# Seven block products (Strassen) for the projection to V in the second layer of a two-layer attention and token-mixing kernel

## The chip, the core and the metric

The kernel runs on one core of a Trainium2 chip. A core has five engines with a queue of instructions each: TensorE (PE, matrix products; its weight loads are listed as PEld), VectorE (DVE), ScalarE (ACT), GpSimd (POOL) and SyncE (SP), which here only issues DMAs. Each engine takes its instructions in the order of the program, and semaphores tie the engines to each other. The metric is the device time in microseconds (us) of one execution, as the median of several runs.

## The reference

Two layers with the same weights; each is sliding-window attention (32 heads of 32, 8 keys at a distance of 2) and a token-mixing MLP.

```python
def _A_ref(x, wqkv, wo):
    qkv = (x @ wqkv).reshape(B, S, 3, H, Dh)        # S = 2048, D = 1024
    ...                                             # windowed softmax attention
    return o @ wo

def _B_ref(x, w1, b1, w2, b2):
    h = _layernorm(x)
    u = _gelu(jnp.einsum("bsd,sf->bdf", h, w1) + b1)  # F = 3584
    y = jnp.einsum("bdf,fs->bds", u, w2) + b2
    return y.transpose(0, 2, 1)

x = x + _A_ref(_layernorm(x), wqkv, wo)             # layer one
x = x + _B_ref(_layernorm(x), w1, b1, w2, b2)
x = x + _A_ref(_layernorm(x), wqkv, wo)             # layer two
x = x + _B_ref(_layernorm(x), w1, b1, w2, b2)
```

The change concerns the last third of `x @ wqkv`, the projection to V, in layer two.

## The kernel before

The 2048 tokens are held as two sets of 1024, even and odd positions (`c = 0, 1`), of eight tiles of 128 tokens each (`i = 0..7`); `cols(c, i)` are the columns of a tile in `hT`, the normalised input with the 1024 features on the partitions (eight blocks `kt`). The stages of a layer follow each other: projection to V, then attention unit by unit (projection to Q and K, scores, mask, values), output projection, the first product of the MLP (`gemm1`) and the second (`gemm2f` in layer one, `gemm2s` in layer two). The two products of the MLP are already done as seven block products each, in half precision (f16), with their weights scaled by a power of two that comes from a bound of the absolute weights. Such a bound is found per partition, stored to DRAM and read back as a broadcast to all partitions (`share_w2`: a small reduction on DVE, the store `mxw` and the broadcast `bcw` on SP); `power_w2` reduces the broadcast on DVE to the scale and its inverse.

- **The order of work.** `chain_(engine, f, ...)` writes out the order on an engine: every call comes behind the engine's call before. `in_order` does the same for PE. In layer one's start, `start_up` has a list for each engine (`pe`, `act`, `dve`, `sp`).
- **V in layer one** runs in `start_up`, tile by tile, with the normalisation of the input. **V in layer two** is `v_proj`: for each tile (c, i) and each half n of the 1024 outputs, eight matmuls 128x128 by 128x512 into a bank of PSUM, then a copy on ACT to `v[c][i]`.
- **`gemm2f`** (layer one). For `i = 0, 1` the products are plain (`tokens`), with the weights `w(0)` and `w(1)`; during these the bounds of the later weights are found: `refill` loads pieces of `w2` into free room of `hT`, ACT's `bounds` makes a bound of each piece, `share(4)` and `share(6)` spread them, and `scaled`, `mix`, `t2` and `t4` make the sums for `i = 2`. For `i = 2..7` there are seven products of 14 matmuls each, with a bank move on ACT between some of them. After each `i` come `quarter` (DVE: scale, add to the residual), `aggregate` (statistics; the store to `xb`), `root` (ACT: reciprocal root) and `normalise` (DVE, then a transposing DMA into `hT`). `seam(0)` at `i = 6` loads the V weights `wv`, `seam(1)` at `i = 7` the first weights of Q and K.
- **Buffers.** `wp` has nine weight buffers, `gop` 14 (the hidden values `g` of the MLP fill them until the sixth product of `i = 7`), `x2p` six; PSUM has eight banks (two `m`, four `s`, two `a`).
- `zero_fill` clears `Pm` (the masked probabilities) and both `qB` on DVE, once in `start_up` and once behind `gemm2f`.

## Time and profile before

| | |
|---|---|
| median of 3 runs | 1207.44 us (1207.15 to 1207.7) |
| the profiled execution | 1208.3 us, span of its instructions 1206.5 us |
| busy, share of the span | PE 98%, DVE 62%, ACT 56%, POOL 10% |
| granted clock of PE | 1.0 over the span |
| V of layer two | 608.4 to 663.8 us |
| `gemm2f`, `i = 0, 1` (`tokens`) | from 432.7 us |
| `gemm2f`, `i = 2` to `7` | from 481.0 us |

The span is the time from the first to the last instruction that the profile shows; times in the prediction are counted from its start. In lines of the order of time, the columns are the start, the length, engine, line and operation, written tile `<-` read tiles, shapes, and in brackets the idle time of the engine before it with what ended it. A line of waits has the engine and what it waited for, the sum, the number of times, and the longest. L1125 is the line of the products of `gemm2f`, L1130 that of its moves on ACT, L1159 `quarter`, L1171 `aggregate`, L1175 `root`, L212 `normalise`, L692 the bounds on ACT, L658 to L661 `share_w2`, L611 any DVE tensor-tensor operation, L226 DMAs that `chain_` issues.

### The profile page before, as it was taken

The numbers are of one execution on the slowest core, as the hardware profiler recorded it, in microseconds if no ns is written. First come the engines' busy times: TensorE is split into PE (matmuls) and PEld (weight loads), VectorE is DVE, ScalarE is ACT, GpSimd is POOL, SyncE is SP. The second block draws the span as 40 slices with busy tenths as digits, with TensorE's granted clock in tenths as the row PEclk, the third lists the DMA queues.
The fourth block names the chain that finished last, engine by engine and source line by source line (L and its number), as shares of the span: only waits on it lengthen the run. The fifth ranks groups of instructions, "written<-read, shape, count | busy, mean of one in ns | idle before, by whom it ended". The sixth has DMA issues, their size and how long they took to land.

```text
span 1206.5 us, 20332 instructions
## 1 busy us (share of the span) xinstructions
PE 1188.3 (98%) x7865; PEld 551.6 (46%) x8004; DVE 751.8 (62%) x1451; ACT 671.2 (56%) x1136; POOL 125.8 (10%) x121
## 2 busy tenths in 40 slices
PE   9999999999999999999999999999999999999998
PEld 4444444444444444444444444444444444444444
DVE  7558887887777546866440688888612322784663
ACT  4457766578878776665433677754543434432332
POOL 0000000281000041000000000002811212100000
PEclk9999999999999999999999999999999999999999
DMA  8922233696776678966520232425855645165521
GB/s 236 157 63 71 79 106 95 211 277 167 205 210 169 206 197 196 223 175 163 160 53 1 65 86 67 121 92 166 279 157 161 199 150 162 48 192 140 157 70 36
DMA packets 248274, 174.01 MB, mean 144 GB/s; under 512 B 48240, under 2 KB 224496, under 8 KB 244848
## 3 DMA queue, kind: packets, MB, share of 16 engines
q1 hardware_dynamic: 248176, 172.69, 51.3%
q8 instruction: 63, 1.03, 0.4%
q14 instruction: 35, 0.29, 0.1%
HBM read 130.17 MB, written 30.43 MB: 133 GB/s over the span
## 4 chain that ended last, share of the span: by engine, by line
PE 94%; DMA 2%; DVE 2%; ACT 1%; issue 1%; DVEq 0%
PE m L400 18%; PE s L771 11%; PE m L516 9%; PE m L771 7%; PE s L975 7%; PE a L771 6%; PE m L385 5%; PE s L1125 4%; PE m L975 4%; PE s L289 3%; PE m L1125 3%; PE a L975 3%; PE s L597 2%; PE a L1125 2%; PE s L431 2%; PE s L1218 2%
## 5 line engine op out<-in xcount | busy, mean ns | idle before, releaser
L400 PE MATMUL m<-hT,wqk 128*128 128x512 bf16 x963 | 223.7, 379 | 6.2 <-issue 4.5
L447 DVE TENSOR_TENSOR Pm<-pc,band 32x640 bf16<-32x640 bf16 x256 | 123.6, 483 | 45.7 <-ACT pc L435 38.9
L400 PEld LDWEIGHTS <-wqk 128*128 128x128 bf16 x1024 | 95.3, 98 | 117.9 <-issue 10.7
L771 PEld LDWEIGHTS <-Sw 128*128 128x128 f16 x832 | 81.4, 98 | 99.4 <-issue 1.3
L516 PE MATMUL m<-wo,oT 128*128 128x512 bf16 x500 | 110.8, 379 | 0.9 <-issue 0.3
L771 PEld LDWEIGHTS <-w 128*128 128x128 f16 (+1 forms) x624 | 61.1, 98 | 73.6
L611 POOL TENSOR_TENSOR T<-h 128x512 f16<-128x512 bf16 x16 | 18.5, 1154 | 613.0 <-DMA xr<-xb 363.9
L411 DVE COPY qB<-qs 32x512 bf16<-32x512 bf16 x136 | 38.2, 281 | 66.3 <-ACT qs L407 63.3
L516 PEld LDWEIGHTS <-oT 128*128 128x128 bf16 x512 | 49.6, 98 | 60.6 <-issue 1.9
L435 ACT ACTIVATE pc<-s,shift 128x320 bf16<-128x320 f32 x128 | 60.9, 532 | 11.7 <-PE s L431 11.7
L771 PE MATMUL s<-T,Sw 128*128 128x512 f16 x288 | 66.2, 379 | 1.1 <-ACT s L780 1.1
L611 DVE TENSOR_TENSOR py<-pz,m 128x512 f32<-128x512 f32 x14 | 9.6, 687 | 91.2 <-PE m L771 62.8
L407 ACT CAST qs<-m 128x512 bf16<-128x512 f32 x64 | 37.5, 586 | 44.4 <-PE m L400 41.6
L404 ACT CAST kT<-m 128x512 bf16<-128x512 f32 x64 | 37.5, 586 | 41.8 <-PE m L400 38.8
L611 POOL TENSOR_TENSOR Pm<-g 128x512 f16<-128x512 bf16 x24 | 28.6, 1209 | 283.1 <-ACT Pm L692 164.3
L385 PE MATMUL m<-wv,hT 128*128 128x512 bf16 x251 | 55.2, 379 | 0.3
L523 DVE TENSOR_TENSOR xn<-m,xr 128x512 bf16<-128x512 f32 x64 | 44.1, 689 | 15.2 <-PE m L516 14.6
L771 PE MATMUL m<-T,Sw 128*128 128x512 f16 x224 | 52.9, 379 | 0.0
L771 PE MATMUL a<-h,w 128*128 128x512 bf16 x224 | 52.9, 379 | 0.0
L611 DVE TENSOR_TENSOR xs<-tq,xs 128x512 bf16<-128x512 f32 (+1 forms) x30 | 21.9, 732 | 49.7 <-ACT tq L1130 32.5
L556 ACT ACTIVATE h<-xn,bi,rs 128x1024 bf16<-128x1024 bf16 x32 | 39.7, 1241 | 23.2 <-DVE bi L542 23.2
L747 ACT ACTIVATE w<-w,cs 128x2048 f16<-128x2048 bf16 x26 | 51.8, 1997 | 0.0
(220 smaller groups left out, 2097.8 us busy)
## 6 DMA issues: line engine op xcount, KB each, us to landing
w<-in_B_w_dram SPq DMA_DIRECT2D x110, 512.0 KB, 6.0
sd<-Sw SPq DMA_DIRECT2D x13, 1024.0 KB, 8.2
Sw<-sd SPq DMA_DIRECT2D x13, 1024.0 KB, 4.9
wqk<-in_A_wqkv_dram SPq DMA_DIRECT2D x16, 512.0 KB, 5.0
xa<-xn SPq DMA_DIRECT2D x32, 256.0 KB, 2.9
xs<-xa SPq DMA_DIRECT2D x32, 256.0 KB, 3.6
Pm<-in_B_w_dram SPq DMA_DIRECT2D x26, 256.0 KB, 6.1
wo<-in_A_wo_dram SPq DMA_DIRECT2D x8, 512.0 KB, 6.2
```

The costliest lines, as they stand in the source:

```text
L385: nc.tensor.matmul(ps[:], lhsT=hT[:, kt, cols(c, i)], rhs=wv[kt // 2][:, kt % 2, n * 512:(n + 1) * 512], start=(kt == 0), stop=(kt == KD - 1))
L400: mm = nc.tensor.matmul(ps[:], lhsT=wts[part][:, kt, (g % 2) * P:(g % 2 + 1) * P], rhs=hT[:, kt, lo:lo + 512], start=(kt == 0), stop=(kt = ...
L435: nc.scalar.activation(out=pc[:, 2 * n:2 * n + 2].rearrange("p t h k -> p (t h k)"), in_=ss[n][:, 0:2 * HG * GW], func=ACT.Exp, scale=scal ...
L447: mm = nc.vector.tensor_tensor(out=Pm[rp, :, s0:s0 + HB, r * KG:r * KG + GW].rearrange("p h t k -> p t h k"), in0=pc[rp], in1=mk, op=ALU.mult)
L516: mm = nc.tensor.matmul(ps[:], lhsT=oT[g][:, cols(c, i)], rhs=wo[n][g // 4][:, g % 4, :], start=(g == 0), stop=(g == NG - 1))
L523: return nc.vector.tensor_tensor(out=xn[:, xs_], in0=pss_["o", n][:], in1=xr[:, xs_], op=ALU.add)
L556: last["ACT"] = nc.scalar.activation(out=h2[c][i][:], in_=xn[:], func=ACT.Identity, bias=t["bi"][:], scale=t["rs"][:])
L611: return eng.tensor_tensor(out=out, in0=a, in1=b, op=op)
L747: return nc.scalar.activation(out=w[:].bitcast(FP16), in_=w[:], func=ACT.Identity, scale=cs[:, fb + 1:fb + 2])
L771: r = nc.tensor.matmul(out, lhsT=lhs[:, k, :], rhs=rhs[k], start=start and k == 0, stop=stop and k == NI - 1, skip_group_check=True)
L975: r = nc.tensor.matmul(out, lhsT=lhs[k], rhs=rhs[k][:, cols_], start=start and k == 0, stop=k == K - 1, skip_group_check=True)
L1125: r = nc.tensor.matmul(out, lhsT=lhs[k], rhs=rhs[k], start=start and k == 0, stop=k == K - 1, skip_group_check=True)
```

## The change

`v_proj` gives way to a class `Sevens`. A pair of token tiles is (0, i) and (1, i): with the two halves of the 1024 features and the two halves of the 1024 outputs, a product of 2x2 by 2x2 blocks, done as seven products of four matmuls each. Two pairs are done in turns (a round), on four banks each. The sums of token blocks (`s_sum`, 512 elements a partition from `hT`, f16) go to tiles `Sv` from `gop`, those of weight blocks (`t_sum`, 1024 elements) to tiles `T2`, `T3`, `T4` from `wp`, and `T1` in place; all on DVE. ACT moves banks between the products and scales the four `wv` tiles to f16; DVE's `put` adds two results to a kept one.

The scale comes in layer one: `start_up` gives ACT eight `bound_wv` (one for each block of `wv`, behind evictions 6 to 13) and DVE `top_wv`. In `gemm2f`, `share_wv` (a store and a broadcast) goes to SP behind `load_w(1)`, and `power_wv` to DVE behind the first `corner_add`. At `i = 7` of `gemm2f` the scalings, `t_sum` and `s_sum` of the first two pairs are put between the steps. The `zero_fill` behind `gemm2f` is split: `Pm` is cleared in the second round, both `qB` in the third. `last_pe` is reset in layer one alone, so that PE's order runs on from V to Q and K in layer two.

```diff
@@ -328,9 +336,19 @@
+        def bound_wv(kt):
+            junk = x2("junk")
+            return nc.scalar.activation(out=junk[:], in_=wv[kt // 2][:, kt % 2, :], func=ACT.Abs,
+                                        accum_out=mxv[:, kt // 4, kt % 4:kt % 4 + 1])
+
+        def top_wv():
+            return nc.vector.tensor_reduce(out=mv2[:], in_=mxv[:], op=ALU.max, axis=AX.X)
+
         rs = [(R_, k) for k in range(9, NT)]
         for k in range(4, NT):
             act.append((E_, k))
+            if 0 <= k - 6 < KD:
+                act.append((bound_wv, k - 6))
             act += rs[:2]
...
         dve.append((zero_fill,))
         dve.append((cast_biases,))
+        dve.append((top_wv,))
...
-    def v_proj(v, c, i, wv, ns):
-        for n in ns:
-            ps = m_tile()
-            for kt in range(KD):
-                nc.tensor.matmul(ps[:], lhsT=hT[:, kt, cols(c, i)], rhs=wv[kt // 2][:, kt % 2, n * 512:(n + 1) * 512],
-                                 start=(kt == 0), stop=(kt == KD - 1))
-            nc.scalar.copy(out=v[c][i][:, n * 512:(n + 1) * 512], in_=ps[:])
+    def share_wv():
+        bcw["v"] = pcp.tile([P, P, 2], FP32, name="bcv", tag="pc")
+        nc.sync.dma_start(out=mxvd[:], in_=mv2[:])
+        return nc.sync.dma_start(out=bcw["v"][:], in_=mxvd[:].partition_broadcast(P))
+
+    def power_wv():
+        chain_("DVE", powers, 0, 1, bcw.pop("v")[:].rearrange("p q c -> p (q c)"), csv, civ)
+
+    class Sevens:
+        def __init__(self, wv):
+            self.wv, self.S, self.T = wv, {}, {}
+
+        def scale(self, j):
+            w = self.wv[j][:]
+            chain_("ACT", lambda: nc.scalar.activation(out=w.bitcast(FP16), in_=w, func=ACT.Identity, scale=csv[:]))
+
+        def b(self, r, c, j):
+            return self.wv[2 * r + j][:].bitcast(FP16)[:, :, c * 512:(c + 1) * 512]
+
+        def t(self, n, j):
+            return self.b(0, 1, j) if n == 1 else self.T[n][:, 2 * j:2 * j + 2, :]
+
+        def t_sum(self, n, j):
+            if n > 1 and n not in self.T:
+                self.T[n] = wp.tile([P, 4, 512], FP16, name=f"T{n}", tag="w")
+            x, y = {3: (self.b(1, 1, j), self.b(0, 1, j)), 1: (self.b(0, 1, j), self.b(0, 0, j)),
+                    2: (self.b(1, 1, j), self.b(0, 1, j)), 4: (self.b(1, 0, j), self.T[2][:, 2 * j:2 * j + 2, :] if n == 4 else None)}[n]
+            chain_("DVE", tt, nc.vector, self.t(n, j), x, y, ALU.subtract)
+
+        def a(self, i, r, c):
+            return hT[:, 4 * c:4 * c + 4, cols(r, i)]
+
+        def s_sum(self, i, n):
+            if i not in self.S:
+                self.S[i] = gop.tile([P, 4, 4, P], FP16, name="Sv", tag="go")
+            q = [self.S[i][:, k] for k in range(4)]
+            x, y, op = [(self.a(i, 1, 0), self.a(i, 1, 1), ALU.add), (q[0], self.a(i, 0, 0), ALU.subtract),
+                        (self.a(i, 0, 0), self.a(i, 1, 0), ALU.subtract), (self.a(i, 0, 1), q[1], ALU.subtract)][n]
+            chain_("DVE", tt, nc.vector, q[n], x, y, op)
+
+        def product(self, out, lhs, rhs, start=True):
+            for k in range(4):
+                r = nc.tensor.matmul(out, lhsT=lhs[:, k, :], rhs=rhs(k // 2)[:, k % 2, :], start=start and k == 0, stop=k == 3,
+                                     skip_group_check=True)
+            return r
+
+        def run(self, v, ahead):
+            A, V = "ACT", "DVE"
+            B = lambda r, c: lambda j: self.b(r, c, j)
+            Tn = lambda n: lambda j: self.t(n, j)
+
+            def move(out, src, sc=None):
+                if sc is None:
+                    return nc.scalar.copy(out=out, in_=src)
+                return nc.scalar.activation(out=out, in_=src, func=ACT.Identity, scale=sc)
+
+            def put(i, r, c, src, z):
+                dst = v[r][i][:, c * 512:(c + 1) * 512]
+                return nc.vector.scalar_tensor_tensor(out=dst, in0=src, scalar=civ[:], in1=z, op0=ALU.mult, op1=ALU.add)
+
+            for p in range(0, NI, 2):
+                pr = (p, p + 1)
+                bk, Z = {}, {}
+                for i in pr:
+                    bk[i] = [t[:] for t in (two("s") + two("s") if i % 2 else two("a") + two("m"))]
+                    in_order(self.product, bk[i][0], self.a(i, 0, 0), B(0, 0))
+                    chain_(A, move, bk[i][2], bk[i][0])
+                for i in pr:
+                    in_order(self.product, bk[i][1], self.S[i][:, 0], Tn(1))
+                    Z[i] = x2("z", [P, 512], FP32)
+                    chain_(A, move, Z[i][:], bk[i][1], civ[:])
+                ahead(p, 0)
+                for i in pr:
+                    in_order(self.product, bk[i][2], self.S[i][:, 1], Tn(2), False)
+                    chain_(A, move, bk[i][3], bk[i][2])
+                for i in pr:
+                    in_order(self.product, bk[i][0], self.a(i, 0, 1), B(1, 0), False)
+                    chain_(A, move, v[0][i][:, 0:512], bk[i][0], civ[:])
+                for i in pr:
+                    in_order(self.product, bk[i][3], self.S[i][:, 2], Tn(3), False)
+                    chain_(V, put, i, 1, 1, bk[i][3], Z[i][:])
+                for i in pr:
+                    in_order(self.product, bk[i][2], self.S[i][:, 3], B(1, 1), False)
+                    chain_(V, put, i, 0, 1, bk[i][2], Z[i][:])
+                ahead(p, 1)
+                for i in pr:
+                    in_order(self.product, bk[i][3], self.a(i, 1, 1), Tn(4), False)
+                    chain_(A, move, v[1][i][:, 0:512], bk[i][3], civ[:])
@@ -1209,6 +1309,7 @@
         load_w(1)
+        chain_("SP", share_wv)
...
         corner_add(0, 0, 1)
+        power_wv()
         in_order(tokens, 0, 1)
...
                 if more:
                     scaled(j, q[j][:, 0], 1, 1)
+                else:
+                    sv[0].scale(0)
                 chain_(A, move, Z[:], pd)
                 if more:
                     scaled(j, q[j][:, 1], 0, 1)
+                else:
+                    sv[0].scale(2)
             in_order(product, pb, weights(S2), [T2k(k) for k in range(K)], False)
...
             corner_add(i, 0, 0)
             if more:
                 scaled(j, U2[j], 0, 0, range(2, 4))
+            else:
+                sv[0].scale(1)
+                sv[0].scale(3)
+                sv[0].t_sum(3, 0)
+                sv[0].t_sum(1, 0)
             in_order(product, pc, weights(S3), NT3, False)
             Y = x2("y", [P, 512], FP32)
             chain_(V, tt, nc.vector, Y[:], Z[:], pc, ALU.add)
             quarter(i, 1, 1, Y[:])
             if more:
                 mix(U2[j], q[j][:, 1], U2[j], ALU.subtract)
+            else:
+                sv[0].t_sum(3, 1)
+                sv[0].t_sum(1, 1)
             in_order(product, pb, weights(S4), B22, False)
             chain_(V, tt, nc.vector, Z[:], Z[:], pb, ALU.add)
             quarter(i, 0, 1, Z[:])
@@ -1355,14 +1469,26 @@
             aggregate(i, 0)
             root(i, 0)
             normalise(i, 0)
+            if not more:
+                for n in range(2):
+                    for m in range(2):
+                        sv[0].s_sum(m, n)
+                for m in range(2):
+                    sv[0].t_sum(2, m)
             in_order(product, pc, weights(A22), [T4k(k) for k in range(K)], False)
         i = NI - 1
         quarter(i, 1, 0, prev)
         aggregate(i, 1)
         root(i, 1)
+        for n in range(2):
+            for m in range(2):
+                sv[0].s_sum(m, 2 + n)
+        for m in range(2):
+            sv[0].t_sum(4, m)
         normalise(i, 1)
...
         else:
-            for i in range(NI):
-                for c in range(DIL):
-                    v_proj(v, c, i, wv, (0, 1))
+            def ahead(p, n):
+                if p == 2 and n == 0:
+                    chain_("DVE", zero_p)
+                elif p == 4 and n == 0:
+                    chain_("DVE", zero_q)
+                elif n and p + 2 < NI:
+                    for m in range(4):
+                        for k in range(2):
+                            sv[0].s_sum(p + 2 + k, m)
+
+            sv[0].run(v, ahead)
...
-        last_pe[0] = None
+        if first:
+            last_pe[0] = None
         for part, n in chunks:
             in_order(qk_chunk, 0, wts, part, n)
...
             fill_wv(wv)
+            sv[0] = Sevens(wv)
 
         gemm2f(g, xa[li], xb, seam)
         qB = new_qB()
-        chain_("DVE", zero_fill)
```

Left out are the declarations of the small tiles, the split of `zero_fill` into `zero_p` and `zero_q`, and the condition under which `top_wv` may be issued (after the last `bound_wv`).

More of the change, by code (lines that the diff above doesn't have):

```diff
@@ L164 @@
     gi = const.tile([P, 1], FP32, name="gi")
+    mxv = const.tile([P, 2, KD // 2], FP32, name="mxv")
+    mv2 = const.tile([P, 2], FP32, name="mv2")
+    csv = const.tile([P, 1], FP32, name="csv")
+    civ = const.tile([P, 1], FP32, name="civ")
     mx0 = const.tile([P, NPRE, DIL, NI // 2], FP32, name="mx0")
@@ L173, in zero_q, with zero_p @@
         return r
+    def zero_p():
+        return nc.vector.memset(Pm[:].rearrange("p h t k -> p (h t k)"), 0.0)
     def zero_fill():
-        nc.vector.memset(Pm[:].rearrange("p h t k -> p (h t k)"), 0.0)
+        zero_p()
         return zero_q()
@@ L182 @@
     mxp = dram.tile([P, NPRE + 1], FP32, name="mxp")
+    mxvd = dram.tile([P, 2], FP32, name="mxvd")
     mxw = [dram.tile([P, 2], FP32, name=f"mxw{n}") for n in range(NI // 2)]
@@ L356, in start_up @@
         qs = {"PE": pe, "ACT": act, "DVE": dve, "SP": sp}
-        need = {cast_biases: lambda: (load_biases,) in done, R_: lambda k: k in mvs, N_: lambda k, h: k in rss, tr: lambda k, hf: (N_, k) in done if k > 1 else (M_, k, hf) in done,
+        need = {cast_biases: lambda: (load_biases,) in done, top_wv: lambda: (bound_wv, KD - 1) in done, R_: lambda k: k in mvs, N_: lambda k, h: k in rss, tr: lambda k, hf: (N_, k) in done if k > 1 else (M_, k, hf) in done,
                 S_: lambda k, cc: (x_load, k) in done,
@@ L1363, in gemm2f @@
         root(i, 1)
+        for n in range(2):
[3 more added lines that the diff above has]
+            sv[0].t_sum(4, m)
         normalise(i, 1)
+    sv = [None]
     NU = NG * DIL
```

## The prediction

> **What bounds the kernel now.** I read the page first (shares of the span, the chain that ended last), then the busy times of the V stage, then the order of time of each engine in two places where the change adds waits: the start of `gemm2f` in layer one (440 to 490 us) and its end (600 to 616 us).

> ```profile
> PE 1188.3 (98%) x7865; PEld 551.6 (46%) x8004; DVE 751.8 (62%) x1451; ACT 671.2 (56%) x1136; POOL 125.8 (10%) x121
> PE 94%; DMA 2%; DVE 2%; ACT 1%; issue 1%; DVEq 0%
> ```

> TensorE (PE) is the bound: 98% busy, and 94% of the last chain. A matmul taken away is worth its pitch, and a wait put before PE costs its whole length. The V stage of layer two, by its busy times:

> ```profile
> 608.40:663.80 55.40, 55.14 (x253) 25.14 (x257) 8.99 (x8) 18.77 (x34) 0.00 (x0) 1.00 0.13 26
> ```

> The five busy columns are PE, weight loads, VectorE (DVE), ScalarE (ACT), GpSimd. PE is full, DVE and ACT mostly idle. 256 matmuls in 55.4 us make a pitch of 0.216 us.

> **What is taken away.** Seven products of 4 matmuls for each of 8 pairs are 224 matmuls instead of 256: 32 x 0.216 = 6.9 us less on PE, all of it on the path.

> **The first wait: the shared bound of the weights.** `share_wv` puts two DMAs on SP behind `load_w(1)`, and `power_wv` waits on DVE for the second one to land. In DVE's order the reduction of `share(4)` stands right behind `power_wv`; on SP, `share(4)`'s own two DMAs stand behind `share_wv`, and the first of them needs that reduction. Before, SP in order of time:

> ```profile
> 444.19 0.80 SPq L660 DMA_DIRECT2D mxw<-mx  x1
> 450.41 0.34 SPq L661 DMA_DIRECT2D bcw<-mxw  x1
> 450.84 7.12 SPq L688 DMA_DIRECT2D hT<-in_B_w_dram  x8
> ...
> 461.10 4.63 SPq L226 DMA_DIRECT2D w<-in_B_w_dram  x4
> ```

> The small store `mxw` is issued behind four big weight loads and only lands 6.2 us later; SP stands until then, and refills and `w(2)` come after. After the change the stores of the V bound take these very places (444.2 and 450.4), and the pair of `share(4)` follows: the broadcast lands 4.6 us after issue (its tile's landings were 4.2 to 5.3), `power_wv` takes 1.2 (the same five steps of `power_w2` ran from 458.45 to 459.68), the reduction 0.2, the store 2.8 to 3.6 with no big load ahead (2.8 at 475.18, 3.6 at 424.99; I take 3.1). So SP reaches the broadcast of `share(4)` 4.6 + 1.2 + 0.2 + 3.1, with some 0.1 of issue, 9.2 us later than before (8.2 to 10.5 by the ends), and the refills and `w(2)` move by as much. What hangs on them, ACT, then DVE:

> ```profile
> 456.38 1.06 ACT L692 ACTIVATE hT<-hT 128x1024 bf16<-128x1024 bf16 x1 [4.58 <-DMA hT<-in_B_w_dram]
> ...
> 486.35 0.73 ACT L1130 ACTIVATE s<-s,bia,cs 128x512 f32<-128x512 f32 x1
> ```

> ```profile
> 474.98 0.17 DVE L658 TENSOR_REDUCE mx<-mx 128x2 f32<-128x14 f32 x1 [1.85 <-ACT hT L692]
> 475.07 1.15 DVE L611 TENSOR_TENSOR qa<-qa 128x1024 f16<-128x1024 f16 x2
> ...
> 484.66 0.21 DVE L1171 BATCH_NORM_AGGREGATE mv<-bn 128x2 f32<-128x12 f32 x1
> ```

> ACT waits 4.58 us for the first refill, then works nearly without a break on the bounds and on `scaled(2)` (which again waits for `w(2)`); its last bound releases DVE at 474.98; DVE runs back to back to 484.87; that aggregate releases `root(1, 0)` on ACT, and behind it stands the move `s<-s` at 486.35, which the third product of `i = 2` accumulates into. The waits of PE show how much slack lies at the end of this chain:

> ```profile
> PE s L1125 <- ACT s L1130: 0.2, 1, 0.2
> ```

> None: PE already waits 0.2 us for that move, at 487.1. So the shift goes through whole: **+9.2 us** (8.2 to 10.5). On the way the second product, which had run 484.1 to 487.1, is paced by DVE's 14 differences `T1` (4.77 us from 476.14, shifted to 485.3 to 490.2); PE then stands still from 490.4 to 496.3, 5.9 us.

> **The seam: the sums in front of the last statistics.** Before, DVE and ACT at the end of `gemm2f`:

> ```profile
> 608.62 0.55 DVE L212 TENSOR_SCALAR kT<-xs,mv,rs 128x1024 bf16<-128x1024 bf16 x1 [0.60 <-ACT rs L1176]
> 609.08 0.75 DVE L1159 SCALAR_TENSOR_TENSOR xs<-m,inv,xs 128x512 bf16<-128x512 f32 x1
> ```

> ```profile
> 610.83 0.29 ACT L1175 ACTIVATE ln<-mv,eps 128x1 f32<-128x1 f32 x1
> ```

> The V stage starts on PE at 608.4 whatever DVE does. In the changed order ACT must do `root(7, 1)` before the first bank move of the V stage, and PE's third product needs that move. `root(7, 1)` needs DVE's last aggregate, and DVE now has in front of it two pairs of `t_sum` (four of 0.69 at a pitch of about 0.65, by the 1024-element f16 tensor-tensor rows), four `s_sum` (0.41 by the 512-element f16 from bf16 rows, pitch 0.34; no row has this strided read) and two more `t_sum`. Step by step in old times: the first two `t_sum` end at 603.1, Y and its quarter at 605.2, the next two 606.5, Z and its quarter, statistics and aggregate 608.9, `root(7, 0)` 609.4, normalise 610.0, four `s_sum` 611.4, two `t_sum` 612.6, the last quarter, statistics and aggregate 614.2, `root(7, 1)` 614.8, the move 615.4. PE has done 16 matmuls of the first two steps by 608.55 + 3.46 = 612.0, plus 0.1 of waiting for the first `s_sum` (610.35 against 610.28). So the third step starts at 615.4: **+3.4 us** (3.0 with overlap, 4.5 if no operation overlaps the next). The stand is 3.3 us in one piece.

> **The clock.** PE's rate after a stand can be read at both ends of the run:

> ```profile
> 1.05 4.02 PE L310 MATMUL s<-warm 128*128 128x512 bf16 x9 [1.05 <-DVE warm L111]
> ```

> ```profile
> 1203.00:1207.00 4.00, 0.00 (x0) 0.00 (x0) 0.00 (x0) 0.00 (x0) 0.00 (x0) 1.00 0.13 35
> 1207.00:1209.00 2.00, 0.00 (x0) 0.00 (x0) 0.00 (x0) 0.00 (x0) 0.00 (x0) 0.71 0.00 0
> ```

> The first nine matmuls took 4.02 us, 0.43 us apart, twice the pitch: 2.1 us lost. After the last matmul (ended 1202.2) the granted clock (the 1.00 and 0.71) was full until 1207 at least and fell before 1209, so a stand of 4.8 us kept it and one of 6.8 us lost it. The 5.9 us of the first wait lie just past the middle of that, so I count one such warm-up, **+2.0 us** (0 to 2.1); the 3.3 us of the seam lie below, 0 (with 2.1 as the bad end). [...]

> **What is covered.** In the V stage each round of two pairs takes 56 x 0.216 = 12.1 us of PE. ACT has 10 moves of 0.57 to 0.68, 6.2 us; DVE 4 `put` of 0.75, 8 `s_sum` of 0.41 and at most one zeroing (2.78 for `Pm`, 3.56 for both `qB`), 9.9 us. A move has three products of 0.86, 2.6 us, for 0.6, so nothing waits; without that cover each of the three dependent steps of a round would cost up to 0.6, 7 us in all. The zeroing (6.3 us from 615 on DVE) leaves the seam, where it cost PE nothing, and lands in rounds with 2 us to spare. The four scalings of `wv` (2.00 each by the 128x2048 row) stand where ACT scaled the next `i` before and idled at `i = 7` (2.4 us before a move, 7.8 after the last corner); the weights were issued at 576.3 and land in about 6. The eight bounds in layer one (1.04 each by the `Abs` row) go to ACT between 36 and 58 us, where it idled 1.1 us in every 1.7; they hold back a normalisation by some 1.5 us, whose transposes landed by 48 and are multiplied at 59; bare they would cost 8.3. On SP the last store and transpose of the seam and two `w2p` loads move by 4 us; the tile is not read for 36 us.

> **Sum.** -6.9 + 9.2 + 3.4 + 2.0 = +7.7 us. The profiled execution took 1208.3 us (span 1206.5), which gives 1216.0; the median of the runs is 0.9 lower, 1207.44, and I forecast 1215.1. About 0.2%, 2.4 us, is what a measurement of this kernel can tell from no change.

> **Rivals.**
> - *The clock stays up* at the first wait: +5.7, 1213.1. For it: 4.8 us kept it. 25%.
> - *It falls at both stands and the landings are at their high ends:* -6.9 + 10.5 + 4.5 + 4.2 = +12.3, 1219.7. 12%.
> - *Faster: the late `w(2)` is hidden.* PE works on `w(0)` and `w(1)` until 481.0, and `w(2)`, landed around 471, would even 9 us late be there in time. If the chain behind it gives way (DVE's 3.2 us of idling at 468, ACT's 5.2 before 484.9), only the seam is paid: -6.9 + 3.4 = -3.5, 1203.9. It decides where less than 3.5 us of the 9.2 reaches PE. Against it: those idle times are themselves waits for this chain, and the last link had no slack. 7%.
> - *Half of it gives way:* within 2.4 us of before. 7%.
> - *The rounds don't run dense:* moves arrive late by 0.3 in each of 12 steps, +3.6 on the forecast, 1218.7. Against it: 2.6 us of cover. 4%.

> **The numbers.** The forecast keeps 45%. Slower by over 0.2%: 45 + 25 + 12 + 4 = 86; same 7; faster 7. The range goes from the upper edge of "half gives way" (1207.4 + 2.4, so 1210) to just below the worst sum, 1219.5; it leaves out the two cases of 7 and part of the 12.

> **What would show it.** Right: SP's `mxw` of `share(4)` issued at about 456.5 instead of 444.2; DVE standing from 442 to 455 on `bcv`; PE idle some 6 us before the third product of `i = 2`, its first matmuls there 0.43 apart; 224 matmuls at 0.216 in the V stage after a stand of 3.3 us on ACT's move. Wrong: `bcv` landing by 446, or PE running through 490 without a gap; then the kernel is faster.

## The result and the profile after

The changed kernel takes 1215.74 us (median of 6 runs, 1215.2 to 1218.24) against 1207.3 us of the kernel before (6 runs, 1206.63 to 1207.7): 1.0074 of the time, with an interval of 1.0061 to 1.0087. It is slower by 8.4 us; 1215.1 was forecast. The profiled execution took 1215.23 us with a span of 1213.5, that is 6.9 and 7.0 more than the one of before.

The page first: PE's busy time, and the granted clock in 40 slices of 30 us.

```profile
PE 1197.1 (99%) x7972; PEld 549.1 (45%) x7972; DVE 779.6 (64%) x1513; ACT 692.6 (57%) x1164; POOL 124.8 (10%) x121
PEclk9999999999999999899999999999999999999999
```

PE's sum is no guide here: this page lists 107 instructions more than the one before, though the change takes 32 away, so records are missing in the one before, and the readings below go by starts and waits. The 8 among the clocks is the one to see, the slice around 500 us. The waits of PE, longest first (engine, tile, line, what ended the wait: sum, times, longest):

```profile
PE s L1225 <- ACT s L1230: 5.8, 1, 5.8
PE m L442 <- ACT m L453: 3.0, 1, 3.0
```

These are the two stands that the prediction named; the first was 0.2 before, the second did not exist. The lines of the code have moved: L1225 are the products of `gemm2f`, L1230 its moves, L442 the products of `Sevens`, L453 its bank moves, L711 any DVE tensor-tensor operation, L735 the reduction in `powers`.

**The first wait.** SP in order of time (L402, L403 are `share_wv`; L760, L761 the pair of `share(4)`; L788 the refills, L234 other loads):

```profile
444.40 1.49 SPq L402 DMA_DIRECT2D mxvd<-mv  x1
449.65 0.34 SPq L403 DMA_DIRECT2D bcv<-mxvd  x1
454.69 0.32 SPq L760 DMA_DIRECT2D mxw<-mx  x1
457.61 0.32 SPq L761 DMA_DIRECT2D bcw<-mxw  x1
458.02 7.41 SPq L788 DMA_DIRECT2D hT<-in_B_w_dram  x8
...
468.39 5.85 SPq L234 DMA_DIRECT2D w<-in_B_w_dram  x4
```

`share_wv` stands where `share(4)` had stood, and `share(4)`'s broadcast is issued 7.2 us later (457.61 against 450.41), and `w(2)` 7.3 later (468.39 against 461.10). On DVE and on ACT the same shift arrives:

```profile
453.41 0.42 DVE L735 TENSOR_REDUCE m<-bcv 128x1 f32<-128x256 f32 x1 [11.93 <-DMA bcv<-mxvd]
...
483.64 1.15 DVE L711 TENSOR_TENSOR qa<-qa 128x1024 f16<-128x1024 f16 x2
...
493.24 0.21 DVE L1271 BATCH_NORM_AGGREGATE mv<-bn 128x2 f32<-128x12 f32 x1
```

```profile
463.67 1.06 ACT L792 ACTIVATE hT<-hT 128x1024 bf16<-128x1024 bf16 x1 [12.14 <-DMA hT<-in_B_w_dram]
...
494.93 0.73 ACT L1230 ACTIVATE s<-s,bia,cs 128x512 f32<-128x512 f32 x1
```

DVE stands 11.9 us for `bcv`, ACT 12.1 us for the first refill (4.58 before), and what comes behind is late by 8.6: DVE's differences 483.64 against 475.07, its aggregate 493.24 against 484.66, ACT's move 494.93 against 486.35. PE in order of time, the third product of before first, then the changed kernel (the second number is the length of the group):

```profile
487.13 3.18 PE L1125 MATMUL s<-T,u 128*128 128x512 f16 x14
```

```profile
480.77 3.19 PE L1225 MATMUL s<-g,w 128*128 128x512 bf16 x14
485.18 4.74 PE L1225 MATMUL s<-g,qa 128*128 128x512 f16 x14 [1.23 <-DVE g L711]
495.70 5.04 PE L1225 MATMUL s<-T,u 128*128 128x512 f16 x14 [5.79 <-ACT s L1230]
```

The third product starts at 495.70 instead of 487.13, and its 14 matmuls take 5.04 us instead of 3.18.

**The seam.** PE, then ACT, where the V stage begins (L1275 is `root`):

```profile
621.30 1.03 PE L442 MATMUL s<-wv,Sv 128*128 128x512 f16 x4
625.32 1.44 PE L442 MATMUL m<-T,Sv 128*128 128x512 f16 x4 [2.98 <-ACT m L453]
626.55 1.91 PE L442 MATMUL s<-T,Sv 128*128 128x512 f16 x4
```

```profile
624.25 0.29 ACT L1275 ACTIVATE ln<-mv,eps 128x1 f32<-128x1 f32 x1 [4.79 <-DVE mv L1271]
...
624.68 0.58 ACT L453 COPY m<-a 128x512 f32<-128x512 f32 x1
```

ACT waits 4.79 us for the last aggregate, and the bank move that PE needs stands behind it. Four matmuls take 1.03 us at full rate; here two groups of four take 1.44 and 1.91. The granted clock shows why. In this trace it is half from 492.66 to 499.49 (6.83 us) and from 625.78 to 629.19 (3.41 us); the windows below are 3.41 us long and laid from these changes (span of time, length, busy PE, weight loads, DVE, ACT, POOL, then the clock):

```profile
489.25:492.66 3.41, 0.66 (x2) 0.14 (x2) 3.34 (x7) 0.00 (x0) 0.00 (x0) 1.00 1.01 202
492.66:496.07 3.41, 0.37 (x1) 0.10 (x1) 3.38 (x10) 2.56 (x6) 0.00 (x0) 0.50 1.20 294
496.07:499.49 3.42, 3.42 (x9) 1.21 (x8) 3.35 (x8) 1.59 (x5) 0.00 (x0) 0.50 1.14 282
...
622.36:625.78 3.42, 0.46 (x3) 0.22 (x3) 3.35 (x9) 1.50 (x5) 0.00 (x0) 1.00 0.35 89
625.78:629.19 3.41, 3.41 (x10) 1.18 (x9) 1.39 (x3) 2.22 (x4) 0.00 (x0) 0.50 0.25 48
```

In the window before 492.66 PE worked 0.66 us and stood for the rest; the clock is half in the next, in which it worked only 0.37, and half again in the one behind that. At the seam it worked 0.46 of 3.42, and the next window is at half. Both stretches at half rate fit one grid of 3.41 us: between them, from 499.49 to 625.78, lie 126.29 us, 37 of these. The V stage as a whole, from its first product to the first of the next stage, before and after:

```profile
608.40:663.65 55.25, 54.99 (x253) 25.05 (x256) 8.99 (x8) 18.77 (x34) 0.00 (x0) 1.00 0.13 26
```

```profile
618.43:671.89 53.46, 50.36 (x225) 22.21 (x224) 34.41 (x62) 25.45 (x43) 0.00 (x0) 0.97 0.12 30
```

It starts 10.0 us late and is 1.8 us shorter; of the 8.2 us left, 7.0 are in the span at the end.

### The profile page after: what moved, and what is told of

Same layout as the page of the kernel before. It is cut to its first block, busy times and chain, and to the rows that moved or that the text cites. A ratio compares the mean times of both kernels' runs of the same rounds, so it can differ in the third digit from the quotient of the medians.

```text
span 1213.5 us, 20522 instructions
## 1 busy us (share of the span) xinstructions
PE 1197.1 (99%) x7972; PEld 549.1 (45%) x7972; DVE 779.6 (64%) x1513; ACT 692.6 (57%) x1164; POOL 124.8 (10%) x121
## 3 DMA queue, kind: packets, MB, share of 16 engines
q8 instruction: 62, 1.02, 0.4%
## 4 chain that ended last, share of the span: by engine, by line
PE 89%; DMA 5%; DVE 2%; SPq 1%; ACT 1%; issue 0%; DVEq 0%
PE m L500 18%; PE s L871 11%; PE m L616 9%; PE s L1075 7%; PE m L871 7%; PE a L871 6%; PE s L1225 5%; PE m L1075 4%; PE s L297 3%; PE a L1075 3%; PE s L697 2%; PE a L1225 2%; PE m L1225 2%; PE s L531 2%; PE s L442 2%; DMA mxd<-mx 2%
## 5 line engine op out<-in xcount | busy, mean ns | idle before, releaser
L500 PE MATMUL m<-hT,wqk 128*128 128x512 bf16 x1024 | 231.8, 380 | 0.0
L500 PEld LDWEIGHTS <-wqk 128*128 128x128 bf16 x1024 | 95.3, 98 | 117.9 <-issue 10.7
L711 POOL TENSOR_TENSOR T<-h 128x512 f16<-128x512 bf16 x16 | 18.4, 1153 | 621.9 <-DMA xr<-xb 372.9
L711 DVE TENSOR_TENSOR py<-pz,m 128x512 f32<-128x512 f32 x14 | 9.6, 687 | 90.4 <-PE m L871 62.1
L711 POOL TENSOR_TENSOR Pm<-g 128x512 f16<-128x512 bf16 x24 | 27.7, 1168 | 283.0 <-ACT Pm L792 164.2
L1075 PEld LDWEIGHTS <-u 128*128 128x128 f16 x336 | 32.8, 98 | 39.7
L711 DVE TENSOR_TENSOR xs<-tq,xs 128x512 bf16<-128x512 f32 (+1 forms) x30 | 21.2, 710 | 45.1 <-ACT tq L1230 27.9
```

Source lines behind the costliest of these rows:

```text
L500: mm = nc.tensor.matmul(ps[:], lhsT=wts[part][:, kt, (g % 2) * P:(g % 2 + 1) * P], rhs=hT[:, kt, lo:lo + 512], start=(kt == 0), stop=(kt = ...
L711: return eng.tensor_tensor(out=out, in0=a, in1=b, op=op)
L1075: r = nc.tensor.matmul(out, lhsT=lhs[k], rhs=rhs[k][:, cols_], start=start and k == 0, stop=k == K - 1, skip_group_check=True)
```

## The experiments

The theory is the prediction's: the product saves 6.9 us, and two orders of work cost more than that, each with a stand of PE and a possible fall of the clock behind it. The rivals: the loss lies in the new work itself (sums, moves, rounds that are not dense, the bounds in layer one), or it has to do with the weights' sharing as such, not with its place. The kernel before took 1207.09 us beside runs 1 to 4 and 1207.34 beside 5 to 7, against 1207.3 beside the changed kernel, so that these totals can be set side by side; run 8 has its own.

**1. The sharing earlier.**

```diff
-        chain_("SP", share_wv)            # gemm2f, behind load_w(1)
...
-        power_wv()                        # gemm2f, behind corner_add(0, 0, 1)
...
+                if fb == 5:               # gemm1 of layer one, behind share(far)
+                    chain_("SP", share_wv)
...
+                if fb == 6:               # behind power(9, 10, ...)
+                    power_wv()
...
-        bcw["v"] = pcp.tile([P, P, 2], FP32, name="bcv", tag="pc")
+        bcw["v"] = x2("bcv", [P, P, 2], FP32)
```

> The sharing of the V bound is moved: the two DMAs go to SP in gemm1 of layer one (block 5), the reduction to the scale to DVE one block later, its broadcast into another buffer pool; all else is the changed kernel. Theory: the wait of 8.8 us at the start of gemm2f and its half-clock stretch (1.9 us) come from this order alone; with it gone the time falls by 10.5 to 11 us, to about 1205, and PE has no wait over 0.3 us at the third product of i = 2. Rival (the first wait comes from the refills or the weight loads being slow in themselves, and the order only shows it): the time stays within 3 us of the changed kernel's 1215.7.

Measured: 1205.68 us (11 runs, 1203.44 to 1209.9), 0.9992 of the kernel before (0.9983 to 1.0002); 10 us less than the changed kernel. No wait of L1225 is left. The profiled run is the longest of the eleven, 1209.9; its waits of PE, and two windows of 3.41 us in `gemm1`:

```profile
PE m L442 <- ACT m L453: 3.0, 1, 3.0
PE s L871 <- ACT s L880: 2.7, 2, 2.1
```

```profile
412.76:416.17 3.41, 1.29 (x7) 0.58 (x6) 3.41 (x7) 3.05 (x4) 0.00 (x0) 1.00 0.91 310
416.17:419.59 3.42, 3.42 (x9) 1.22 (x8) 1.38 (x3) 2.95 (x5) 0.00 (x0) 0.50 0.95 257
```

The stand at the seam is the same 3.0 us. The wait of `gemm1` on ACT, 1.1 us in the profile before (L771 there), has grown to 2.7 in this run, 2.1 of it in one piece, and the clock fell behind it: PE stood 2.12 us of the window, and the next reads 0.50. That costs 1.6 us of stand and 1.7 of clock. The mean clocks of the eleven runs go from 1.000 (1203.44) to 0.997 (1209.21 and 1209.9), which fits that some runs pay this and some do not; only the profiled one can be looked into. At 1.000 not even a fall behind the seam, one window at half rate, would have room (an estimate: 1.7 of 1201.7 us lost would read 0.999).

**2. The root of the last tile later.**

```diff
         quarter(i, 1, 0, prev)
         aggregate(i, 1)
-        root(i, 1)
...
-        normalise(i, 1)
+        sv.append(lambda: (root(NI - 1, 1), normalise(NI - 1, 1)))
...
+                if p == 0 and n == 0:     # ahead(0, 0): behind the first four moves
+                    sv.pop()()
```

> Only the seam is changed: the last root and normalise of gemm2f are issued behind the four moves of the first two steps of the V stage instead of ahead of them. Theory: the stand of 3.0 us at the third product goes down to 0.7 (the two T2 sums on DVE still end about 0.6 us late) and the half-clock stretch behind it, worth 1.5 us, goes too: 3.5 to 4 us less, about 1212. Rival (DVE's sums, not ACT's order, hold the third product): it falls by less than 1 us.

Measured: 1212.11 us (5 runs, 1210.53 to 1212.56), 1.0041 (1.0028 to 1.0053). The wait of L442 is gone, and the first wait is as it was (5.8 us). The V stage now:

```profile
619.03:667.71 48.68, 48.56 (x225) 21.86 (x224) 34.22 (x62) 25.54 (x43) 0.00 (x0) 1.00 0.16 33
```

It takes 48.68 us against 53.46: the seam costs 4.8 us, more than the 3.4 of the prediction. PE is busy for 48.56 of them, so the rounds are dense.

**3. Both.** The two edits together.

> Both edits together: the bound shared in gemm1, the last root of gemm2f behind the first moves. Theory: the two costs add, so about 1215.7 - 10.7 - 3.7 = 1201.3, that is 6 us below the kernel before, nearly the whole 6.9 us of the 32 matmuls that are left out. Rival (part of the loss lies in the rounds themselves, in moves that arrive late or in the added bounds on ACT): it stays above 1204.

Measured: 1200.41 us (5 runs, 1199.66 to 1202.54), 0.9948 (0.9935 to 0.9962): faster than the kernel before by 6.7 us, and than the changed one by 15.3. The V stage takes 48.68 us again. With neither stand, what is left is 55.25 - 48.68 = 6.6 us, the products' own gain. The two repairs alone gave 10.1 and 3.6, which adds up to 13.7, and together 15.3. Falls of the clock in `gemm1`, of which the profiled run of the first alone has one, may eat a part there; that is not shown. The profiled run of this one had a wait of 1.3 us at the same place in `gemm1`, and kept its clock (1.00 here and in the next window):

```profile
409.76:413.17 3.41, 2.11 (x11) 0.87 (x9) 3.41 (x6) 2.88 (x4) 0.00 (x0) 1.00 0.93 312
```

**4. The sharing alone, in the kernel before.** The V stage of eight products stays; the two DMAs and the five steps on DVE are put where the change has them, on a constant, and nothing uses their result.

```diff
         load_w(1)
+        chain_("SP", share_wv)            # mv2 is set to 1.0 once
...
         corner_add(0, 0, 1)
+        power_wv()
```

> The kernel before, with only the two DMAs and the five small DVE steps of the shared V bound added at the changed kernel's places in gemm2f (on a constant instead of a bound; the result is not used). Theory: this alone costs the 8.8 us of the first wait and about 2 us of half clock, so 1217.5 to 1218.5. Rival (the wait needs the rest of the change, such as the bounds on ACT in the first stage or the moved clears): within 2 us of 1207.3.

Measured: 1217.29 us (4 runs, 1216.6 to 1217.53), 1.0085 (1.0072 to 1.0099): 10.2 us more than the kernel before, for two small DMAs and five small steps, none of them used. Waits of PE (L1138 and L1143 are products and moves of `gemm2f` here, L624 DVE's tensor-tensor), and the window of the shorter one with the next:

```profile
PE s L1138 <- ACT s L1143: 5.2, 1, 5.2
...
PE s L1138 <- DVE g L624: 1.8, 1, 1.8
```

```profile
483.15:486.57 3.42, 1.65 (x6) 0.57 (x6) 3.11 (x9) 3.42 (x8) 0.00 (x0) 1.00 0.02 0
486.57:489.98 3.41, 3.41 (x9) 1.13 (x8) 3.41 (x10) 1.65 (x3) 0.00 (x0) 0.50 0.45 23
```

The first loss needs nothing of the change but the sharing; that it is a matter of place is shown by 1 and 8. Here even the stand of 1.8 us ahead of the second product was followed by half rate: 1.77 us idle in the window, 0.50 in the next.

**5. PE kept busy in the first wait.**

```diff
             in_order(product, pd, weights(S1), T1)
+            if i == 2:
+                in_order(keep_busy, bk[1][0])   # 25 matmuls ident x g, not used
```

> The changed kernel with 25 idle matmuls (the identity times a tile of g, into a bank that nothing reads before it is overwritten) behind the second product of i = 2, so that PE multiplies through the first wait instead of standing. The wait itself stays. If the 1.9 us behind the stand are a matter of the clock and of PE's idleness alone, the third product still starts near 495.7, now at full rate with no half-clock stretch there, and the kernel takes 1.9 less: 1215.7 - 1.9 = 1213.8. If something else slows these first matmuls (operands, banks, transfers), they stay 0.43 apart and the time stays at 1215.7 or above; if the idle matmuls end after ACT's move, up to 1 us is lost again. The fall at the seam (625.8 to 629.2) stays either way.

Measured: 1215.27 us (4 runs, 1212.14 to 1216.21), 1.0056 (1.0039 to 1.0073). PE in order of time (L1395 are the idle matmuls):

```profile
487.05 5.34 PE L1225 MATMUL s<-g,qa 128*128 128x512 f16 x14 [2.08 <-DVE g L711]
492.23 5.56 PE L1395 MATMUL a<-g,ident 128*128 128x512 bf16 x25
497.62 3.19 PE L1225 MATMUL s<-T,u 128*128 128x512 f16 x14
```

The third product runs at full rate (3.19 us instead of 5.04), so the half rate behind the stand comes from the stand. The total did not fall by the expected 1.9. In this run the chain came later, and ACT's move ended at 497.5 instead of 495.7:

```profile
496.80 0.73 ACT L1230 ACTIVATE s<-s,bia,cs 128x512 f32<-128x512 f32 x1
```

The idle matmuls ended with it, so they did not hold the third product. The wait ahead of the second product grew to 2.1 us (1.2 in the changed kernel), and the product itself took 5.34 us (4.74 there). The run's mean clock of 0.997 leaves room for two stretches of 3.41 us at half rate, an estimate (3.4 of 1214.5 us lost). One lies at the seam, where two groups of four matmuls took 1.86 and 1.51 us; that the other lies in the second product is the author's reading of its 5.34 us. The run whose mean clock was 1.000 took 1212.14, those at 0.997 and 0.998 took 1214.85 to 1216.21.

**6. PE kept busy at the seam.**

```diff
                 ahead(p, 0)
+                if p == 0:
+                    in_order(self.keep_busy, bk[1][3])   # 12 matmuls of the first operands, not used
```

> The changed kernel with 12 idle matmuls (12 x 0.216 = 2.6 us) behind the second product of the first round of the V stage, into a bank that is overwritten later, so that PE hardly stands at the seam. In every run so far the full-rate stretches are whole multiples of 3.41 us, and a stretch at half rate follows a 3.41 us window in which PE stood 1.8 us or more, never one in which it stood 1.4 or less. If the clock is decided so, window by window, the half-rate stretch at 625.8 disappears and the time falls by 1.5 to 1.7: 1214.1. If the stand of 3.0 us was not the cause (the prediction counted none, by a 4.8 us stand that kept the clock at the end of the run), the time stays at 1215.7.

Measured: 1215.05 us (4 runs, 1214.07 to 1216.88), 1.0064 (1.0049 to 1.0079). PE at the seam (L448 are the idle matmuls, L459 is the bank move), and the V stage:

```profile
624.68 2.75 PE L448 MATMUL s<-wv,hT 128*128 128x512 f16 x12
627.84 1.02 PE L442 MATMUL m<-T,Sv 128*128 128x512 f16 x4 [0.40 <-ACT m L459]
```

```profile
620.94:672.73 51.79, 51.28 (x238) 22.96 (x237) 34.44 (x62) 25.37 (x43) 0.00 (x0) 1.00 0.16 31
```

The third step still comes 6.9 us behind the first, but at full rate: 1.02 for four matmuls. The stage takes 51.79 us instead of 53.46. So of the 4.8 us of the seam the stand is 51.79 - 48.68 = 3.1, and the clock 53.46 - 51.79 = 1.7. In the median of the total only 0.7 of the expected 1.6 is seen; the profiled run lost more in the first wait (its third product of `i = 2` started 15.9 us after the first one, against 14.9 in the changed kernel).

**7. The seven products alone**, without bounds or sharing, and with the root later as in 2.

```diff
-            if 0 <= k - 6 < KD:
-                act.append((bound_wv, k - 6))
...
-        dve.append((top_wv,))
...
-        chain_("SP", share_wv)
...
-        power_wv()
...
+    nc.vector.memset(csv[:], 1.0)
+    nc.vector.memset(civ[:], 1.0)
```

> Seven products alone: the bounds of the V weights on ScalarE in layer one, their sharing over SP and the powers on VectorE are left out (the scale of the V weights is a constant 1.0, so the output is not scaled as the change has it), and root and normalise of the last tile stand behind the first moves of the V stage. If the bounds in layer one cost nothing, as the prediction has it, and the early sharing costs nothing either, this takes what the kernel with both repairs takes, 1200.4, or up to 1 less for the waits in gemm1 of 1.3 against 0.9 and of attention of 1.3 against 0.9. If the eight bounds hold PE back in layer one by the 1.5 us that they delay a normalisation, it takes 1198.9 or less. By the pitch alone it would be 1207.1 - 6.9 = 1200.2.

Measured: 1200.16 us (4 runs, 1199.63 to 1203.29), 0.9945 (0.993 to 0.9959), no different from 1200.41 with bounds and sharing. The eight bounds on ACT in layer one, and a sharing at a place with room, cost nothing that can be measured.

**8. The sharing later.** To the other side of the first wait, with the root later as in 2.

```diff
-        chain_("SP", share_wv)            # gemm2f, behind load_w(1)
...
-        power_wv()                        # behind corner_add(0, 0, 1)
...
             load_x(i)
+            if i == 4:
+                chain_("SP", share_wv)
...
             normalise(i - 1, 1)
+            if i == 5:
+                power_wv()
```

> The changed kernel with the whole sharing of the V bound moved out of the first wait to the other side: its two DMAs on SP behind the load of x in i = 4 of gemm2f, its five steps on VectorE behind the normalisation in i = 5, with root and normalise of the last tile behind the first moves of the V stage as in the version with both repairs. If the first wait was a matter of order alone (two DMAs and a landing ahead of those of share(4)), the third product of i = 2 starts where it did before, near 487, no half-rate stretch is left, and the kernel takes 1200.2, as with the seven products alone; the waits of gemm1 go back to the 0.3 to 1.1 of before. If what cost there was the DMA's or the steps' own work, or if the steps (1.2 us of VectorE in i = 5, one wait of 4 us for the broadcast if it lands late) delay the products there, it takes 1201.5 to 1205.

Measured: 1204.71 us (6 runs, 1202.98 to 1207.17). On the chip of this run the kernel before took 1212.85 (11 runs, 1209.58 to 1215.59), so the ratio counts: 0.9931 (0.9915 to 0.9948). That is the lowest of the versions, with an interval that overlaps those of 3 and 7. The second and third product of `i = 2`:

```profile
490.67 3.19 PE L1225 MATMUL s<-g,qa 128*128 128x512 f16 x14
493.69 1.67 PE L1225 MATMUL s<-T,u 128*128 128x512 f16 x7
```

No stand between them (they come 6.6 us later than before; `gemm1` has waits of up to 2.8 us here, and the run's mean clock of 0.999 leaves room, by an estimate, for one stretch of 3.41 us at half rate, 1.7 of 1205.5 us lost; where it lies is not shown). The broadcast landed 4.6 us after its issue, with no one waiting. The sharing costs by its place, not as such. Why the kernel before is 5.5 us slower on this chip is not known.

## Why the prediction was right, and where it was not

The terms of the sum, as forecast and as measured (profiled executions):

| | forecast | measured | from |
|---|---|---|---|
| 32 products less | -6.9 | -6.6 | V stage 55.25 to 48.68 (2, 3, 7) |
| the first wait | +9.2 | +8.6 | third product 487.13 to 495.70 |
| clock behind it | +2.0 | +1.5 | V stage 10.0 late, less 8.6 |
| seam, the stand | +3.4 | +3.1 | 51.79 less 48.68 (6) |
| seam, the clock | 0 | +1.7 | 53.46 less 51.79 (6) |
| the rest | 0 | -1.2 | 8.2 late at the end of the V stage, 7.0 at the end |
| sum | +7.7 | +7.1 | span +7.0 |

- **The first wait** came by the mechanism forecast, SP to ACT and DVE to PE, and went through whole. Its size was made of errors that made up for each other, which is luck. The broadcast of the bound was issued 0.8 us ahead of where `share(4)`'s had stood (449.65 against 450.41), `bcv` landed 3.7 after issue (4.6 taken), `power_wv` and the reduction took 1.2 and 0.15 as taken, the store 2.9 (3.1 taken), so that SP was 7.2 late and not 9.2; but `w(2)` came slower behind it (ACT waited 3.6 us for its pieces, 2.1 before), so that DVE and ACT were 8.6 late. The stand was 5.8 us (5.9 forecast). That it is order alone is shown by 4 (the loss without any use of the bound) and by 1 and 8 (no such wait with the sharing elsewhere).
- **The clock at the first wait.** One warm-up of 2.0 was counted; the third product took 1.9 longer (5.04 against 3.18). Of it 1.5 was left at the V stage. 5 shows that it is the stand: with PE busy the product takes 3.19.
- **The seam.** `root(7, 1)` held ACT's first move as forecast; 2 takes it away with one edit.
- **The step that failed** is the clock at the seam, counted at 0 because a stand of 4.8 us at the end of the run had kept the clock. The length of that stand did not carry over. In windows of 3.41 us laid back from the change at 1207.40, the end of the run before reads:

```profile
1200.57:1203.98 3.41, 1.62 (x20) 1.16 (x17) 0.98 (x3) 0.67 (x1) 0.00 (x0) 1.00 0.29 106
1203.98:1207.40 3.42, 0.00 (x0) 0.00 (x0) 0.00 (x0) 0.00 (x0) 0.00 (x0) 1.00 0.06 12
1207.40:1208.50 1.10, 0.00 (x0) 0.00 (x0) 0.00 (x0) 0.00 (x0) 0.00 (x0) 0.51 0.00 0
```

  PE stopped half-way through one window (1.79 us idle of 3.41), stood through the whole of the next, and the clock fell at that one's end. The 4.8 us were the rest of one window and nearly all of a second. At the seam 2.96 of the 3.0 us fell into one window, and the next was at half rate. The prediction put the stand of 3.3 us below one of 4.8 that had kept the clock; in the traces 2.12 us idle in one window (1) was already followed by half rate.
- **The rest** was forecast at 0: the rounds (48.56 of 48.68 us busy) and the bounds in layer one (7) cost nothing, as argued (ACT's idle time of 1.1 in every 1.7 us begins at 44 in the profile before, not at 36, which made no difference). The -1.2 behind the V stage was not tried; 0.5 of it lies between V and the output projection and 0.8 at the end, and the runs of the kernel before themselves spread over 1 us.

- **The rivals.** That the clock stays up at the first wait, that the late `w(2)` is hidden, and that the rounds are not dense are each excluded by a row above: 5.04, the stand of 5.8, and 48.56 of 48.68. That half gives way is excluded by the total, 8.4 us. The rival with a fall at both stands came half true: the clock fell at both, but the landing was early (3.7 us) and not late.

In the profiled executions the sum came out 0.6 us below the forecast because the missing 1.7 was more than made up by terms that were taken too large, the first wait, its clock and the stand of the seam, and by the rest. That is luck in the number. By the medians the change is 8.4 us, 0.7 above the forecast: the profiled execution of before lay 1.0 above its median, that of the changed kernel 0.5 below.

## What to carry to other kernels

A small transfer that a chain waits for costs what stands behind it in its queue, not its bytes: two DMAs of a bound cost 10.2 us at one place and nothing that could be measured at others, so put such a thing where its queue and its reader have no dependent work right behind. When a stage that feeds an in-order engine (here the last statistics into ACT) is followed by a new stage whose first steps need that engine, put the stage's first moves ahead of the tail of the old one. Add to a new stand of PE the clock that it may cost behind it (here 1.9 us behind 5.8 and 1.7 behind 3.0), and read that from the granted clock in short windows of the trace, not from the length of another stand.
